# A fused attention and two-FFN kernel: first pass from one list in another order, 14 VectorE operations on GpSimd, later conversions at other steps

## The chip, the cores and the metric

The kernel runs on one core of one Trainium2 chip. The metric is the device time of one execution in microseconds (us); the kernel before takes 734.96 us, the median of three runs.

A core has five engines, each with its own queue of instructions that it works off in order: PE (TensorE) multiplies matrices, DVE (VectorE), ACT (ScalarE) and POOL (GpSimd) work on tiles, and SP (SyncE) here only starts DMA transfers. An engine waits at the head of its queue until the tiles that the instruction needs are ready and the buffers that it writes are free.

## The reference

Two softmax attentions in a row, then two feed-forward networks (FFNs):

```python
def sm_attn(qq, kk, vv):
    s = scale * np.matmul(qq, kk.transpose(0, 1, 3, 2))
    s = s - np.max(s, axis=-1, keepdims=True)
    a = np.exp(s)
    a = a / (np.sum(a, axis=-1, keepdims=True) + 1e-09)
    return np.matmul(a, vv)
p_packed = sm_attn(p, k, v)          # 32 packed tokens look at 576 tokens
out = sm_attn(q, p_packed, p_packed) # 576 tokens look at the 32 packed ones
...
x = ...reshape(B * S, H * D)         # 2304 tokens of 512 channels
g = softplus(x @ w_in);  x = g @ w_out        # first FFN, 2048 hidden channels
h = x @ w_in2;           h * sigmoid(h) @ w_out2   # second FFN, 2048 hidden channels
```

There are 4 batches, 8 heads of 64 channels and 576 tokens in a batch. `q`, `k`, `v`, `p` and the first FFN's `w_in` are drawn eight times as large as usual. All arrays are float32; the weights reach the kernel as 64-bit words, from which it makes float32.

## The kernel before

**Tiling.** The 2304 tokens are 8 blocks of 288 columns; block 2b and 2b + 1 belong to batch b. The first FFN's 2048 hidden channels are 16 tiles of 128, worked in 4 passes of 4 tiles: a unit is one block with the 4 hidden tiles of a pass (the first two blocks are cut into units of 2 tiles), a step is one hidden tile of a unit or one output tile of the unit before. There are 128 steps, 32 to a pass, so step 32 begins the second pass. One matrix instruction of PE is called a product.

**One step s of the first FFN.** `emit_in(s)` (L533) makes `h`, six products of 128x288: float32 accuracy comes from splitting each operand into a high part and a low part and multiplying three pairs. `act_scalar` (L550) has ACT take the softplus of `h` and round it to the high part `gh`; `act_vector` (L563) has DVE subtract for the low part `gl` (L564). `emit_out(s)` (L570) makes one output tile `y` of the unit before, twelve products (L596; in the first 8 steps plain float32 products from `gf`, L589). `finish_out` (L602) copies or adds `y` to the sum `ya` (L608 on ACT, L610 and L612 on DVE). `h` has two PSUM buffers, and so has `y`: the `h` of step s cannot start before the softplus and the `gl` of step s - 2 have read theirs. In the first 28 steps the softplus goes into a tile `gt`, so that the bank is free without `gl`; from step 28 on it stays in the bank, and the bank is free only when `gl` is made.

**Attention in the first pass.** `att1(b)` (L363) is the attention of batch b's packed tokens: scores of `kt` and `pz` (L376), two row maxima `top` (L382, DVE), two exponentials (L388, ACT), transposes through PE (L397) and their copies `et` (L402, L404, ACT), products with the values `vt` (L412), the division into `px` (L437 to L440, DVE), its transpose (L445) and the copy `pt` (L449). `att2(blk)` (L451) is the attention of a block: scores (L460), a transpose into `tr` and its maximum, difference, exponential, sum, a small addition, reciprocal and product (L469 to L483: DVE, the exponential ACT), the transpose `tb` (L485), its high part in `ax` (L490, ACT) and its low part (L492, DVE). `packed(b, qs)` (L500) multiplies the packed values with a part of `w_in` into `vw` (L509 PE, L517 ACT, L525 DVE); the FFN's `h` is then made from `ax` and `vw`. All of it shares two PSUM buffers, `psa`.

**Conversions.** `conv_w` (L155) makes float32 weights of the first FFN from raw words `wraw`: a scaling on ACT (L147, L149), a shift (L165) and one or two ORs (L168, L171) on DVE, and for `w_out` the high part on ACT (L183) and the low part `lo` (L186), on DVE at first, on POOL from step 32 on. From step 32 on the second FFN's weights are converted too and stored to DRAM for later: pairs of `w_in2` tiles (steps in the table `I2`; shift and OR L212 to L217 DVE, sums L231 POOL, high part L240 ACT, low part L246 POOL, store `wd` L254) and tiles of `w_out2` (table `O2`; sums L287 POOL, high part L272 ACT, low part L276 POOL, and for each second tile the rest L297 ACT and L301 POOL; stores `od` L280 and `td` L304). All loads and stores stand in SP's queue in the order in which they are written.

**What sets the order.** The order of each engine's queue is the order in which the program issues the operations. Each piece of work is a generator (`Item`) that stops at yields named after points of a step ("PE", "D1", "A1", ...). `start()` (L749) writes out the beginning by hand; `plan_all()` (L681) then puts items and loads on an agenda by step numbers, and `run_steps` (L813) goes through the steps and runs, at each point, all items that wait for it.

`warm(n)` (L739) issues n products of the identity with itself, filler work for PE; there are 54 of them in the first pass. After the 128 steps comes the second FFN (`second`), which the change does not touch.

Of the kernel before, what the change touches and what calls it, by code (L numbers as in the profile page):

```python
# [49 lines left out]
def body(ctx, tc, kT, vv, qT, pT, wi1, wo1, wi2, wo2, out):  # L50
# [26 lines left out]
    def setup():  # L77
        make_identity(nc, ident)
        nc.scalar.preload_act_table_set("exp_and_others")
# [14 lines left out]
    class Item:  # L94
# [9 lines left out]
        def first(self, point):  # L104
            assert self.due == point
            self.due = next(self.gen, None)
# [48 lines left out]
    def conv_w(k, n, signed=False):  # L155
# [29 lines left out]
        eng = nc.gpsimd if "x" in banks else nc.vector  # L185
# [152 lines left out]
    kts, vts, qts, pts = {}, {}, {}, {}  # L338

    def load_k(b):  # L340
        pz = att.tile([P, NK, NP], F32, name="pz", bufs=2)
        nc.sync.dma_start(out=pz, in_=pT[b])
        nc.gpsimd.tensor_scalar(out=pz, in0=pz, scalar1=SCALE, scalar2=None, op0=ALU.mult)
# [19 lines left out]
    def att1(b):  # L363
# [87 lines left out]
    def att2(blk, last=False):  # L451
# [18 lines left out]
        if blk == 3:  # L470
            yield "next"
# [7 lines left out]
        nc.vector.tensor_scalar(out=mx[:, 1], in0=mx[:, 1], scalar1=1e-9, scalar2=None, op0=ALU.add)  # L479
        nc.vector.reciprocal(out=mx[:, 1], in_=mx[:, 1])  # L480
        if blk == 2:
            yield "D2"
        nc.vector.tensor_tensor(out=tr, in0=tr, in1=mx[:, 1].unsqueeze(2).to_broadcast(wide), op=ALU.mult)  # L483
        tb = att.tile([P, NR, N0], F32, name="tb", bufs=1)
        nc.vector.transpose(tb, tr.rearrange("q (r g) p -> q r (g p)", r=NR))  # L485
        if last:
            yield "next"
# [4 lines left out]
        nc.vector.tensor_tensor(  # L492
# [7 lines left out]
    def packed(b, qs):  # L500
# [18 lines left out]
        if b == B - 1 and qs == (1,):  # L519
            yield "next"  # L520
            yield "D1"
        else:
            yield "D"
# [26 lines left out]
    def act_scalar(s, h):  # L550
# [7 lines left out]
        gt = h if s >= base(1) - 4 else att.tile([P, N0], F32, name="gt", bufs=2)  # L558
# [4 lines left out]
    def act_vector(s, gt, gh, gl):  # L563
        nc.vector.tensor_tensor(out=gl, in0=gt, in1=gh.bitcast(F32), op=ALU.subtract)  # L564
# [37 lines left out]
    def finish_out(u, dm, y):  # L602
# [3 lines left out]
        if u == FIRST[blk]:  # L606
            if dm % 2 or u < 3:
# [56 lines left out]
    I2 = (1, 4), (10, 13), (19, 22), (33, 34), (40, 44), (52, 54), (64, 69), (75, 78)  # L664
    O2 = 3, 6, 12, 15, 21, 25, 31, 36, 42, 46, 57, 62, 68, 70, 81, 83
# [15 lines left out]
    def plan_all():  # L681

        for n, s in (("i", 4), 11), (("i", 5), 19), (("i", 6), 26), (("i", 7), 28):
            when[n] = s
        for n, s in (("o", 4), 17), (("o", 5), 30), (("o", 6), 32), (("o", 7), 34):
            when[n] = s
        for f in range(1, NPASS - 1):
            for d, s in enumerate((5, 9, 26, 28)):
                when["i", GJ * f + GJ + d] = base(f) + s
            for d, s in enumerate((11, 17, 18, 24)):  # L690
                when["o", GJ * f + GJ + d] = base(f) + s
        for (k, n), s in when.items():
            ring = RING[k]
            free = last_use(k, n - ring) if n >= ring else 0
# [28 lines left out]
        for b in range(1, B):  # L723
            t = 8 * b
            if b > 1:
                plan_load(lambda b=b: load_k(b), t - 16)
                plan_load(lambda b=b: load_v(b), t - 13)
                plan(Item(att1(b)), (t - 10, t - 9, t - 7, t - 6, t - 5))
            for i in range(2):
                plan_load(lambda i=i, b=b: load_q(2 * b + i), max(0, t - 11 + i))  # L730
            plan(Item(att2(2 * b)), (t - 4, t - 3, t - 2))
            last = b == B - 1
# [540 lines left out]
```

## Time and profile before

| | |
|---|---|
| Three runs, median (lowest to highest) | 734.96 us (734.56 to 735.1) |
| The profiled execution, its own time | 735.33 us |
| Its span in the trace | 733.5 us |
| PE busy | 720.1 us, 98% of the span |
| DVE busy | 532.0 us, 73% |
| ACT busy | 395.3 us, 54% |
| POOL busy | 383.0 us, 52% |

The span is what the trace covers, from the first to the last instruction; 1.8 us of the execution's own time lie around it. The busy times of the engines overlap, so the share says only which engine has hardly any room. How long an engine stood still, and for whom, is in the list of waits; where that was is in the timeline, which shows instruction for instruction when it started, how long it took and, in brackets, how long its engine had stood still before it and what it had waited for.

### The profile page before, as it was taken

What the parts mean: (1) busy time and instruction counts of PE and PEld (TensorE: products, weight loads), DVE (VectorE), ACT (ScalarE), POOL (GpSimd) and SP (SyncE); (2) the same over time, 40 slices, a digit from 0 to 9 for tenths busy, and PEclk for the clock granted to TensorE, in tenths of its full rate; (3) what the DMA queues carried; (4) which work ended last, traced back from release to release, by engine and by line L of the source; (5) the groups of instructions that cost most, each with busy time, mean ns of one, the idle gap of its engine ahead of it and who ended that gap; (6) DMA issues with size and microseconds to landing.
All of it is one profiled execution on the core that took longest, in us unless ns stands there. A gap on an engine that the chain in (4) does not pass through costs nothing.

```text
span 733.5 us, 14136 instructions
## 1 busy us (share of the span) xinstructions
PE 720.1 (98%) x5336; PEld 686.9 (94%) x5336; DVE 532.0 (73%) x943; ACT 395.3 (54%) x785; POOL 383.0 (52%) x338
## 2 busy tenths in 40 slices
PE   8998999997999999999999999999999999999998
PEld 6776989997999999999999999999999999999997
DVE  3888888898878888855855567787567776745557
ACT  3667886766756657555535453544553353443341
POOL 0000000558736836447007657679766769865655
PEclk9999999999999999999999999999999999999999
DMA  8965060567787584562928978788987787897842
GB/s 335 359 229 180 9 258 2 202 232 287 285 303 271 236 324 185 202 245 88 369 81 255 311 238 276 238 259 269 324 263 245 245 265 244 300 309 234 257 127 101
DMA packets 78915, 173.22 MB, mean 236 GB/s; under 512 B 6400, under 2 KB 52992, under 8 KB 76288
## 3 DMA queue, kind: packets, MB, share of 16 engines
q1 hardware_dynamic: 78848, 172.33, 68.9%
q8 instruction: 42, 0.69, 0.4%
q14 instruction: 25, 0.20, 0.1%
HBM read 136.13 MB, written 36.18 MB: 235 GB/s over the span
## 4 chain that ended last, share of the span: by engine, by line
PE 78%; DVE 11%; ACT 4%; DMA 2%; issue 2%; POOL 1%; SPq 0%; DVEq 0%; POOLq 0%
PE y L976 23%; PE y L596 18%; PE h L547 9%; PE pB L919 7%; PE pA L919 7%; PE pC L919 7%; PE pD L919 3%; PE psa L509 2%; DVE wx L165 1%; PE y L589 1%; DMA wraw<-wi 1%; DMA td<-tmp 1%; DVE gl L564 1%; DVE raw L214 1%; DVE wx L168 1%
## 5 line engine op out<-in xcount | busy, mean ns | idle before, releaser
L596 PE MATMUL y<-gh,w 128*128 128x288 f32 x960 | 211.9, 297 | 0.2 <-DVE ya L610 0.2
L596 PEld LDWEIGHTS y<-gh,w 128*128 128x128 f32 x960 | 160.3, 188 | 12.8 <-issue 11.8
L976 PE MATMUL y<-G,w 128*128 128x384 f32 x840 | 164.4, 334 | 0.2 <-DVE acc L991 0.2
L976 PEld LDWEIGHTS y<-G,w 128*128 128x128 f32 x840 | 147.2, 188 | 0.5 <-DVE acc L991 0.5
L596 PE MATMUL y<-gl,w 128*128 128x288 f32 x480 | 141.4, 295 | 0.0
L547 PE MATMUL h<-ax,vw 128*128 128x288 f32 x768 | 125.1, 299 | 5.4 <-DVE gl L564 4.5
L547 PEld LDWEIGHTS h<-ax,vw 128*128 128x128 f32 x768 | 108.8, 188 | 9.1 <-DVE gl L564 6.3
L958 POOL TENSOR_TENSOR G<-sums,G 128x384 fp32r<-128x384 f32 x76 | 87.9, 1178 | 35.1 <-ACT G L954 21.0
L950 POOL TENSOR_TENSOR sums<-tmp 128x384 f32<-128x384 f32 x47 | 56.5, 1224 | 91.9 <-ACT tmp L1163 90.6
L596 PEld LDWEIGHTS y<-gl,w 128*128 128x128 f32 x480 | 90.1, 188 | 0.0
L559 ACT ACTIVATE h<-h 128x288 f32<-128x288 f32 x100 | 38.9, 389 | 50.6 <-PE h L547 48.3
L564 DVE TENSOR_TENSOR gl<-h,gh 128x288 fp32r<-128x288 f32 x100 | 45.0, 450 | 28.4 <-ACT gh L560 28.3
L186 POOL TENSOR_TENSOR w<-wx,w 128x512 fp32r<-128x512 f32 x10 | 14.0, 1402 | 93.7 <-ACT w L183 93.7
L1159 ACT ACTIVATE tmp<-tmp 128x384 f32<-128x384 f32 x24 | 12.6, 526 | 80.5 <-DVE tmp L1090 80.5
L1090 DVE TENSOR_TENSOR tmp<-tmp,pB 128x384 f32<-128x384 f32 x48 | 26.4, 550 | 40.2 <-PE pB L919 36.1
L612 DVE TENSOR_TENSOR ya<-y,ya 128x288 f32<-128x288 f32 x104 | 46.6, 450 | 10.2 <-PE y L596 10.2
L1090 DVE TENSOR_TENSOR G<-tmp,G 128x384 fp32r<-128x384 f32 x61 | 45.4, 745 | 11.4 <-ACT G L1160 6.1
L287 POOL TENSOR_TENSOR tmp<-tmp 128x256 f32<-128x256 f32 x32 | 23.8, 755 | 50.0 <-DVE tmp L217 25.5
L1119 ACT ACTIVATE tmp<-pA 128x384 f32<-128x384 f32 x24 | 11.8, 492 | 68.3 <-PE pA L919 68.3
L919 PE MATMUL pC<-xc,w 128*128 128x384 f32 x240 | 48.1, 334 | 0.0
L919 PE MATMUL pB<-xc,w 128*128 128x384 f32 x240 | 48.1, 334 | 0.0
L991 DVE TENSOR_TENSOR ya<-y,ya 128x384 f32<-128x384 f32 x70 | 38.4, 552 | 11.1 <-PE y L976 10.8
(144 smaller groups left out, 1399.4 us busy)
## 6 DMA issues: line engine op xcount, KB each, us to landing
w<-wd SPq DMA_DIRECT2D x84, 512.0 KB, 4.5
w<-td SPq DMA_DIRECT2D x96, 256.0 KB, 3.9
w<-od SPq DMA_DIRECT2D x72, 256.0 KB, 4.1
wd<-whl SPq DMA_DIRECT2D x8, 1792.0 KB, 8.8
wraw<-wi SPq DMA_DIRECT2D x16, 512.0 KB, 6.3
wraw<-wo SPq DMA_DIRECT2D x16, 512.0 KB, 9.1
raw<-wi SPq DMA_DIRECT2D x16, 512.0 KB, 6.1
raw<-wo SPq DMA_DIRECT2D x16, 512.0 KB, 5.3
```

Source lines behind the costliest of these rows:

```text
L287: sub = lambda o, a, b: nc.gpsimd.tensor_tensor(out=o, in0=a, in1=b, op=ALU.subtract)
L547: nc.tensor.matmul(h, lhsT=w, rhs=x, start=(i == 0), stop=(i == len(mm) - 1))
L559: nc.scalar.activation(out=gt, in_=h, func=AF.Softplus)
L564: nc.vector.tensor_tensor(out=gl, in0=gt, in1=gh.bitcast(F32), op=ALU.subtract)
L596: nc.tensor.matmul(y, lhsT=w[:, c], rhs=g, start=(j == js[0] and m == 0), stop=(j == js[-1] and m == 2))
L612: nc.vector.tensor_tensor(out=acc, in0=y, in1=acc, op=ALU.add)
L919: nc.tensor.matmul(out, lhsT=a, rhs=b, start=start and not i, stop=not start and i == len(mm) - 1, skip_group_check=True,)
L950: eng.tensor_tensor(out=sum_of(q), in0=a, in1=b, op=op)
L958: eng.tensor_tensor(out=u[:, 1], in0=sum_of(q), in1=u[:, 0].bitcast(F32), op=ALU.subtract)
L976: nc.tensor.matmul(y, lhsT=w, rhs=g, start=not m, stop=m == len(mm) - 1)
L991: vec = lambda o, x, z, op=ALU.add: nc.vector.tensor_tensor(out=o, in0=x, in1=z, op=op)
L1090: add = lambda o, i, j, op=ALU.add: nc.vector.tensor_tensor(out=o, in0=i, in1=j, op=op)
```

## The change

The first pass (steps 0 to 31 and what comes ahead of them) is no longer planned by steps. One list, `SCRIPT`, has a token for each operation or next stage of an item, in the order in which they are issued: `a1.b` is the next stage of `att1(b)`, `a2.k` of `att2` of block k, `v.b.i` of `packed`, `w.k.n` of `conv_w`; `in.s`, `sp.s`, `gl.s`, `out.s` and `fin.u.d` are `emit_in`, softplus and rounding, `gl`, `emit_out` and `finish_out`; `L...` are loads, `warm.n` is filler, `table` is the load of ACT's first table. New yields let stages that were one be issued apart. The first batch's `pz` is loaded through ACT's queue instead of SP's, and the table load now stands behind it.

Fourteen operations of DVE go to POOL (`ON_POOL`): the difference `sub` of blocks 2, 4, 5, 6 and 7, the product `mul` of blocks 2 and 5 and the low part `low` of blocks 0 and 2 (nine of 128x576), `lo` of weight 3 (128x512), `gl` of steps 14 and 21 (128x288), and the small addition `eps` of blocks 4 and 7. Which first copies of `y` go to ACT is now a list, `BY_SCALAR`; two more of them are on DVE than before.

From step 32 on, the conversions of weights for the last two passes move: in the second and the third pass the `w_in` tiles from steps 5, 9, 26, 28 to 7, 9, 26, 29 and the `w_out` tiles from 11, 17, 18, 24 to 11, 19, 17, 24. In the tables of the second FFN's weights six of the eight pairs in `I2` and two tiles in `O2` have other steps, and the store of a pair is asked for one step later.

```diff
     def setup():
         make_identity(nc, ident)
-        nc.scalar.preload_act_table_set("exp_and_others")
...
-        eng = nc.gpsimd if "x" in banks else nc.vector
+        eng = nc.gpsimd if "x" in banks else engine("lo", n)
...
+    def load_p(b):
+        pz = pzs[b] = att.tile([P, NK, NP], F32, name="pz", bufs=2)
+        (nc.sync if b else nc.scalar).dma_start(out=pz, in_=pT[b])
+        nc.gpsimd.tensor_scalar(out=pz, in0=pz, scalar1=SCALE, scalar2=None, op0=ALU.mult)
...
-        nc.vector.tensor_tensor(out=tr, in0=tr, in1=mx[:, 0].unsqueeze(2).to_broadcast(wide), op=ALU.subtract)
+        yield "D2" if blk == 3 else "D"
+        engine("sub", blk).tensor_tensor(out=tr, in0=tr, in1=mx[:, 0].unsqueeze(2).to_broadcast(wide), op=ALU.subtract)
...
-        nc.vector.tensor_tensor(
+        engine("low", blk).tensor_tensor(
             out=ax[:, NR:, cols], in0=tb, in1=ax[:, :NR, cols].bitcast(F32), op=ALU.subtract
         )
...
-        gt = h if s >= base(1) - 4 else att.tile([P, N0], F32, name="gt", bufs=2)
+        gt = h if s >= IN_BANK else att.tile([P, N0], F32, name="gt", bufs=2)
...
-        nc.vector.tensor_tensor(out=gl, in0=gt, in1=gh.bitcast(F32), op=ALU.subtract)
+        (engine("gl", s) if s < IN_BANK else nc.vector).tensor_tensor(out=gl, in0=gt, in1=gh.bitcast(F32), op=ALU.subtract)
...
-            if dm % 2 or u < 3:
+            if 4 * u + dm in BY_SCALAR:
...
-    I2 = (1, 4), (10, 13), (19, 22), (33, 34), (40, 44), (52, 54), (64, 69), (75, 78)
-    O2 = 3, 6, 12, 15, 21, 25, 31, 36, 42, 46, 57, 62, 68, 70, 81, 83
+    I2 = (1, 5), (10, 13), (20, 22), (32, 34), (42, 44), (52, 54), (65, 66), (72, 75)
+    O2 = 3, 6, 12, 15, 21, 25, 30, 36, 45, 46, 57, 62, 68, 70, 81, 83
...
-            for d, s in enumerate((5, 9, 26, 28)):
+            for d, s in enumerate((7, 9, 26, 29)):
                 when["i", GJ * f + GJ + d] = base(f) + s
-            for d, s in enumerate((11, 17, 18, 24)):
+            for d, s in enumerate((11, 19, 17, 24)):
                 when["o", GJ * f + GJ + d] = base(f) + s
...
-            plan_load(lambda jp=jp: store_i(jp), b + 7)
+            plan_load(lambda jp=jp: store_i(jp), b + 8)
...
+    ON_POOL = (("sub", 4), ("lo", 3), ("sub", 7), ("low", 2), ("sub", 6), ("mul", 2), ("sub", 2), ("gl", 21), ("low", 0), ("sub", 5), ("gl", 14), ("eps", 4), ("mul", 5), ("eps", 7), )
+    IN_BANK = 28
+    BY_SCALAR = (0, 1, 2, 3, 4, 5, 6, 17, 22, 25, 27, 30, 31, 32, 33, 34, 35, 36)
+    engine = lambda *x: nc.gpsimd if x in ON_POOL else nc.vector
...
+        warm.12 Lp.0 table.exp_and_others Lk.0 Lw.i.0 Lv.0 Lw.i.1 Lq.0 Lw.o.0 Lw.o.1 a1.0 Lp.1 Lq.1 Lk.1
+        Lw.i.2 Lw.i.3 Lw.o.2 Lw.o.3 w.i.0 a1.0 w.i.0 w.i.0 a1.0 a1.0 a1.0 warm.8 a1.0 a1.0 a1.0 a1.0 a1.0
...
     with tc.manual_schedule():
-        start()
         plan_all()
+        first_pass()
         run_steps(NS)
```

In the fences below a row is an instruction of the engine's queue with its line, its tiles (the number behind a name tells tiles of the same name apart) and the size that it writes; x4 stands for four such in a row.

At the very start DVE's queue makes the row maxima of batch 0 (`sm`, L382), two float32 weights (`wx` and `wraw`, L165 and L171) and the packed values `px`. Before:

```order
L382 TENSOR_REDUCE sm_123<-psa_138 128x1
L382 TENSOR_REDUCE sm_123<-psa_139 128x1
L165 TENSOR_SCALAR wx_175<-wraw_110 128x512
L171 SCALAR_TENSOR_TENSOR wraw_110<-wraw_110,wx_175 128x512
L165 TENSOR_SCALAR wx_251<-wraw_115 128x512
L437 TENSOR_SCALAR sm_123<-psa_209 128x2
L438 RECIPROCAL sm_123<-sm_123 128x2
L440 TENSOR_TENSOR px_255<-psa_209,sm_123 128x128
L171 SCALAR_TENSOR_TENSOR wraw_115<-wraw_115,wx_251 128x512
```

Now, with the same lines under other numbers (L384 is the maximum, L164 the shift, L170 the OR, L443 to L446 `px`), in DVE's queue:

```order
L384 TENSOR_REDUCE sm_103<-psa_140 128x1
L164 TENSOR_SCALAR wx_176<-wraw_127 128x512
L170 SCALAR_TENSOR_TENSOR wraw_127<-wraw_127,wx_176 128x512
L384 TENSOR_REDUCE sm_103<-psa_141 128x1
L443 TENSOR_SCALAR sm_103<-psa_211 128x2
L444 RECIPROCAL sm_103<-sm_103 128x2
L446 TENSOR_TENSOR px_255<-psa_211,sm_103 128x128
L164 TENSOR_SCALAR wx_257<-wraw_132 128x512
L170 SCALAR_TENSOR_TENSOR wraw_132<-wraw_132,wx_257 128x512
```

The second weight's shift has moved from ahead of `px` to behind it, and the first weight's shift and OR from behind the second maximum to ahead of it.

At batch 2 PE's queue has the scores of `att1(2)` (L376), the transposes of its two exponentials (L397, `e_723` and `e_725`), and around them `h` (L547) and `y` (L589) of the first steps. Before:

```order
L376 MATMUL psa<-kt,pz 32x288 x16
L589 MATMUL y<-gf,wraw 128x288 x4
L547 MATMUL h<-ax,vw 128x288 x12
L589 MATMUL y<-gf,wraw 128x288 x2
L547 MATMUL h<-ax,vw 128x288 x6
L589 MATMUL y<-gf,wraw 128x288 x2
L397 MATMUL psa<-ident,e_723 128x128 x4
L397 MATMUL psa<-ident,e_723 64x128
L397 MATMUL psa<-ident,e_725 128x128 x4
L397 MATMUL psa<-ident,e_725 64x128
L547 MATMUL h<-ax,vw 128x288 x6
L589 MATMUL y<-gf,wraw 128x288 x2
```

Now (L378 scores, L399 transposes, L546 `h`, L588 `y`, L414 the products with the values), in PE's queue:

```order
L378 MATMUL psa<-kt,pz 32x288 x16
L546 MATMUL h<-ax,vw 128x288 x12
L588 MATMUL y<-gf,wraw 128x288 x2
L399 MATMUL psa<-ident,e_726 128x128 x4
L399 MATMUL psa<-ident,e_726 64x128
L588 MATMUL y<-gf,wraw 128x288 x2
L399 MATMUL psa<-ident,e_728 128x128 x4
L399 MATMUL psa<-ident,e_728 64x128
L546 MATMUL h<-ax,vw 128x288 x6
L588 MATMUL y<-gf,wraw 128x288 x2
L546 MATMUL h<-ax,vw 128x288 x6
L414 MATMUL psa<-vt,et 32x65 x40
```

Four products of `y` have moved from behind the scores to ahead of them, one `h` of six products from ahead of the transposes to behind them, and two products of `y` stand between the transposes.

At steps 49 to 52, in the second pass, DVE's queue has `gl` (L564), the sum `ya` (L612) and the conversions of weights for the third pass (L165 to L171). Before:

```order
L165 TENSOR_SCALAR wx_2375<-wraw_2196 128x512
L168 SCALAR_TENSOR_TENSOR wx_2375<-x_2349,wx_2375 128x512
L171 SCALAR_TENSOR_TENSOR wx_2375<-x_2349,wx_2375 128x512
L564 TENSOR_TENSOR gl_2359<-h_2351,gh_2358 128x288
L612 TENSOR_TENSOR ya_92<-y_2362,ya_92 128x288
L165 TENSOR_SCALAR wx_2414<-wraw_2233 128x512
L168 SCALAR_TENSOR_TENSOR wx_2414<-x_2388,wx_2414 128x512
L171 SCALAR_TENSOR_TENSOR wx_2414<-x_2388,wx_2414 128x512
L564 TENSOR_TENSOR gl_2398<-h_2390,gh_2397 128x288
L612 TENSOR_TENSOR ya_92<-y_2401,ya_92 128x288
```

Now (L164 to L170 the conversion, L563 `gl`, L611 `ya`), in DVE's queue:

```order
L164 TENSOR_SCALAR wx_2375<-wraw_2195 128x512
L167 SCALAR_TENSOR_TENSOR wx_2375<-x_2349,wx_2375 128x512
L170 SCALAR_TENSOR_TENSOR wx_2375<-x_2349,wx_2375 128x512
L563 TENSOR_TENSOR gl_2359<-h_2351,gh_2358 128x288
L611 TENSOR_TENSOR ya_92<-y_2362,ya_92 128x288
L563 TENSOR_TENSOR gl_2396<-h_2388,gh_2395 128x288
L611 TENSOR_TENSOR ya_92<-y_2399,ya_92 128x288
L164 TENSOR_SCALAR wx_2440<-wraw_2274 128x512
L167 SCALAR_TENSOR_TENSOR wx_2440<-x_2414,wx_2440 128x512
L170 SCALAR_TENSOR_TENSOR wx_2440<-x_2414,wx_2440 128x512
L563 TENSOR_TENSOR gl_2424<-h_2416,gh_2423 128x288
```

The second of the two conversions has moved back by one step: a step without a conversion now lies between them.

## Rows read from the trace of the kernel before

**Rows 1.** Page, part 1: each engine's busy us (share of the span) xinstructions

```profile
PE 720.1 (98%) x5336; PEld 686.9 (94%) x5336; DVE 532.0 (73%) x943; ACT 395.3 (54%) x785; POOL 383.0 (52%) x338
```

**Rows 2.** Waits of PE: line waited for: us in total, times, longest us

```profile
PE h L547 <- DVE gl L564: 4.5, 5, 2.0
...
PE psa L445 <- DVE px L440: 1.0, 1, 1.0
PE h L547 <- ACT gt L559: 1.0, 1, 1.0
PE psa L509 <- DVE vw L525: 0.8, 1, 0.8
PE psa L412 <- ACT et L404: 0.4, 1, 0.4
```

**Rows 3.** Timeline, 13 to 126 us: start, us, engine, line, out<-in [idle before <-releaser]

```profile
13.31 0.43 DVE L165 TENSOR_SCALAR wx<-wraw 128x512 int32<-128x512 int32 x1 [2.93 <-DMA wraw<-wi]
...
14.48 0.30 PE L445 MATMUL psa<-ident,px 128*128 128x128 f32 x1 [1.01 <-DVE px L440]
...
123.27 0.95 PE L547 MATMUL h<-ax,vw 128*128 128x288 f32 x6
...
125.64 0.95 PE L547 MATMUL h<-ax,vw 128*128 128x288 f32 x6
```

**Rows 4.** Timeline of PE and ACT, 48 to 60 us

```profile
48.56 1.43 PE L376 MATMUL psa<-kt,pz 64*32 64x288 f32 x32
49.92 2.21 PE L589 MATMUL y<-gf,wraw 128*128 128x288 f32 x8
...
56.75 1.28 ACT L559 ACT_TABLE_LOAD   x1
...
58.51 1.06 PE L547 MATMUL h<-ax,vw 128*128 128x288 f32 x6 [0.96 <-ACT gt L559]
```

**Rows 5.** Timeline of SP's queue and of POOL, 153 to 163 us

```profile
153.60 0.38 SPq L304 DMA_DIRECT2D td<-tmp  x1
...
162.16 0.74 POOL L287 TENSOR_TENSOR tmp<-tmp 128x256 f32<-128x256 f32 x1 [4.72 <-DMA td<-tmp]
```

**Rows 6.** Timeline, 168 to 184 us

```profile
171.20 0.69 DVE L168 SCALAR_TENSOR_TENSOR wx<-x,wx 128x512 int32<-128x512 int32 x1 [2.26 <-ACT x L149]
...
173.03 1.06 PE L547 MATMUL h<-ax,vw 128*128 128x288 f32 x6 [1.34 <-DVE gl L564]
...
173.08 2.39 POOL L301 TENSOR_TENSOR tmp<-tmp 128x1024 fp32r<-128x1024 f32 x1
...
173.26 2.49 DVE L165 TENSOR_SCALAR wx<-wraw 128x512 int32<-128x512 int32 x1
...
177.69 1.07 PE L547 MATMUL h<-ax,vw 128*128 128x288 f32 x6 [2.02 <-DVE gl L564]
...
180.97 1.06 PE L547 MATMUL h<-ax,vw 128*128 128x288 f32 x6 [0.63 <-DVE gl L564]
```

**Rows 7.** DVE by line and shape, 0 to 124 us: xcount | busy us, mean ns | idle

```profile
L564 DVE TENSOR_TENSOR gl<-gt,gh 128x288 fp32r<-128x288 f32 x20 | 8.8, 441 | 3.0 <-ACT gh L560 3.0
...
L474 DVE TENSOR_TENSOR tr<-tr,mx 128x576 f32<-128x576 f32 x8 | 6.1, 758 | 0.3
...
L186 DVE TENSOR_TENSOR w<-wraw,w 128x512 fp32r<-128x512 f32 x4 | 2.7, 673 | 0.0
```

**Rows 8.** POOL by line and shape, whole span

```profile
L276 POOL TENSOR_TENSOR ohl<-tmp,ohl 128x512 fp32r<-128x512 f32 x16 | 21.8, 1365 | 0.0
L301 POOL TENSOR_TENSOR tmp<-tmp 128x1024 fp32r<-128x1024 f32 x8 | 19.4, 2431 | 0.3 <-ACT tmp L297 0.3
...
L343 POOL TENSOR_SCALAR pz<-pz 128x128 f32<-128x128 f32 x4 | 2.5, 620 | 45.6 <-DMA pz<-pT 45.6
```

**Rows 9.** Instructions of L165 and L1090: ns min/median/max, first and last start

```profile
L165 DVE TENSOR_SCALAR wx<-wraw x32: 385/418/2656, 9.2 to 281.5; 128x512 int32<-128x512 int32 x32
...
L1090 DVE TENSOR_TENSOR G<-tmp,G x61: 546/559/1412, 378.5 to 707.3; 128x384 fp32r<-128x384 f32 x61
```

More of the change, by code (lines that the diff above doesn't have):

```diff
@@ L102, in run, with step @@
                     self.due = next(self.gen, None)
-        def first(self, point):
-            assert self.due == point
+        def step(self):
+            assert self.due
             self.due = next(self.gen, None)
@@ L423, in att1 @@
         exp(0)
+        yield "A1"
         exp(1)
@@ L518, in packed @@
             vs.append(v)
[L519 to L523, printed above, removed]
+        yield "D"
         for i, (q, v) in enumerate(zip(qs, vs)):
@@ L693, in plan_all @@
             ring = RING[k]
-            free = last_use(k, n - ring) if n >= ring else 0
+            free = last_use(k, n - ring)
             load = max(s - 5, free)
@@ L721, in plan_all @@
             plan_load(lambda r=r: load_s(r), base(3) + 24)
[L723 to L732, printed above, removed]
-            plan(Item(att2(2 * b + 1, last)), (t - 3,) + (t - 2,) * (b == 1) + (t - 1, t) + (t + 1,) * last)
         for (b, qs), s in vstep.items():
-            plan(Item(packed(b, qs)), (s, s + 1) if b == B - 1 and qs == (1,) else (s,))
+            if s >= base(1):
+                plan(Item(packed(b, qs)), (s,))
     def warm(n):
@@ new lines, in body, with first_pass, act, send @@
+    """
+    def first_pass():
+        items, made, ys = {}, {}, {}
+        for b in range(B):
+            items[f"a1.{b}"] = Item(att1(b))
+            for i in range(2):
+                items[f"a2.{2 * b + i}"] = Item(att2(2 * b + i))
+                items[f"v.{b}.{i}"] = Item(packed(b, (i,)))
+        items["v.0.2.3"] = Item(packed(0, (2, 3)))
+        for n in range(2 * GJ):
+            for k in "io":
+                items[f"w.{k}.{n}"] = Item(conv_w(k, n, n < 2 + (k == "i")))
+        def act(s):
+            made[s] = act_scalar(s, made[s])
+        def send(s):
+            for y in emit_out(s):
+                ys[y[:2]] = y
+        calls = {
+            "Lp": load_p, "table": nc.scalar.preload_act_table_set, "Lk": load_k, "Lv": load_v, "Lq": load_q, "Lw": load_w, "warm": warm, "sp": act, "out": send,
+            "in": lambda s: made.update({s: emit_in(s)}), "gl": lambda s: act_vector(s, *made[s]),
+            "fin": lambda u, dm: finish_out(*ys.pop((u, dm))),
+        }
+        for t in SCRIPT.split():
+            if t in items:
+                items[t].step()
+            else:
+                name, *args = t.split(".")
+                calls[name](*(int(a) if a.isdigit() else a for a in args))
+        assert not ys
+        for k, n, s in LATE:
+            plan(items[f"w.{k}.{n}"], s)
@@ L813, in run_steps @@
     def run_steps(end):
-        for s in range(end):
+        for s in range(base(1), end):
             if s == base(1):
@@ L835, in run_steps @@
             r = act_scalar(s, h)
[L836 removed]
+            ys = emit_out(s)
             go("PE2")
[L838 to L844 removed]
             go("A1")
```

129 lines of the change are left out of this document (36 added, 93 removed).

## The prediction, made before the changed kernel was run

> **What bounds the kernel now.** I read the busy table first: the matrix unit PE is busy for 98% of the span, so this is a kernel of one engine, and a change can give only what PE idles or does needlessly [rows 1]. The change adds and drops no matrix instruction: the same tiles are multiplied, and the 54 filler products of `warm` stay 54. So the next view is the list of what PE waited for [rows 2]. Its rows are the whole purse: 4.5 us in five waits for `gl`, and some 4 us of waits of a microsecond or less. Those small ones lie in the first pass, which ends where PE begins step 32, at 123.27 us; the `gl` waits lie behind it [rows 2, 3]. A kernel with none of these waits would be 8 to 9 us faster, no more.
>
> Then I read the places in order of time. At 13 to 15 us VectorE (DVE) stands 2.93 us for a weight's DMA, and the small operations that make `px` stand behind that in DVE's queue; PE waits 1.01 us for `px` [rows 3]. At 48 to 59 us the scores of batch 2 are done at 49.99, yet PE waits 0.96 us at 58.51 for a softplus: DVE comes to the row maxima late, so ScalarE's exponentials are late, and the table load of 1.28 us and the softplus come behind them [rows 4]. Shortly behind it stands a wait of 0.4 for `et`, and at 70 us one of 0.8 for `vw` [rows 2].
>
> The large hole is in the second pass. GpSimd (POOL) waits 4.72 us for the store of `td`, issued at 153.60, and goes on at 162.16 [rows 5]. Its sums are then late; ScalarE waits for them and is late with the scaled weight; DVE waits 2.26 us for that weight, and `gl`, which stands behind it, frees PE's bank 1.34 us too late. Then two weight conversions follow in neighbouring steps (49 and 50), and the shift of the second takes 2.49 us: it ends only when POOL's operation of 2.39 us, begun at 173.08, has ended. For that PE waits 2.02 and 0.63 us more [rows 6]. The two other `gl` waits, 4.5 − 3.99 = 0.5 us together [rows 2], come behind such shifts in the third pass and later.
>
> **The change part by part.** *Fourteen operations from DVE to POOL.* Nine are of 128x576, one of 128x512, two of 128x288, two tiny. By DVE's rows that takes 9 × 0.758 + 0.673 + 2 × 0.441 = 8.4 us off DVE [rows 7]. Two more copies of `y` come to DVE from ScalarE, at `gl`'s size about 0.9 us. POOL has no such operation before step 32; its nearest rows are 1.365 us for 128x512 and 2.431 for 128x1024, so I estimate 1.50 for 576 columns and 0.9 for 288: 9 × 1.50 + 1.4 + 1.8 = 16.7 us, in a stretch where it had only the four scalings of `pz` to do [rows 8]. Each result comes 0.75 us later than DVE would give it, and is hidden only where its consumer is late anyway.
>
> *Another order of the first pass.* (a) Start: `px` now stands ahead of the shift that waits for the DMA, and two filler products fill the time until then. Against that, the first weight's shift and OR (a median of 0.42 us [rows 9], and about 0.67 as `lo` of that width) now stand between the two row maxima, which delays the second exponential. Bounds: the whole 1.01 us gained, or 0.5 lost. I take 0.2 gained. (b) Batch 2: between the scores and the `h` that waited, the order drops four `y` products (eight records, 2.2 us) and moves one `h` group behind; the 7.6 us of PE work there (49.99 to 58.51 less 0.96) becomes some 4.6 to 4.9 [rows 4]. What must fit in is the chain of two maxima, the second exponential, table load and softplus. I count maxima and exponential like DVE's operations of 576 columns and the softplus like `gl`: 3 × 0.76 + 1.28 + 0.44 = 4.0 us, if DVE is free when the scores end. It is: four 576-column operations have left its queue ahead of the maxima and one copy has come in, 4 × 0.758 − 0.44 = 2.6 us net, and the scores come 2 us later. So the 0.96 us goes, and the 0.4 for `et` behind it; the cover left is under 1 us. (c) The wait of 0.8 for `vw`: PE arrives earlier by what (b) gave, DVE's queue from `px` to it is about 1 us shorter; I take 0.3 of it as gained, bounds 0 and 0.8. (d) New: the `h` of batch 3's first block (block 6) hangs on a copy, table load, softplus, rounding, `ax` and its low part: 3 × 0.44 + 1.28 + 2 × 0.76 = 4.1 us behind the product that starts the chain. PE now has two products and an `h` for it, also some 4 us: 0.3 us lost, bounds 0 and 1. Sum of the first pass: 0.2 + 1.0 + 0.4 + 0.3 − 0.3 = 1.6 us, bounds −1.1 (the start 0.5 worse, `et` and `vw` as before, (b) eaten up by (d) and as much again elsewhere) and 3.2.
>
> *Conversions at other steps.* The two conversions of steps 49 and 50 become 49 and 51 (the same distance apart in the third pass). The `td` store stands behind the same raw load in SyncE's queue, so POOL's late start stays, and with it the first 1.34. But step 50 is now free of a conversion, so DVE catches up ahead of the next shift: the 2.02 and 0.63 go. In their place come four conversions in a row at steps 51 to 54, under POOL's same long operations. A step of PE has 125.64 − 123.27 = 2.37 us [rows 3]; one with a conversion needs 0.42 + 2 × 0.67 + 2 × 0.44 = 2.6 of DVE. I put 0.8 us of new waiting there, bounds 0 and 4. The 0.5 of the later places goes, less 0.1. Sum: 2.65 − 0.8 + 0.4 = 2.25 us, bounds −1.4 and 4.5.
>
> *Nothing* I give to the table load and the load of `pz` that now stand in ScalarE's queue: the twelve filler products cover both. Nothing either to the loads moved in SyncE's queue: the closest is the key tile of batch 3, asked for when batch 2's values are used up, at some 62 us, and needed at some 73; without that cover it would cost what it lands late.
>
> DVE work on SBUF tiles beside a busy POOL is the price I trust least. The trace shows it: the shift has a median of 418 ns and a maximum of 2656, and a product of two SBUF tiles 546 at least and 1412 at most [rows 9]. The Trainium skill, "SBUF — State Buffer", section "Who interferes with whom", says that DVE operations with two SBUF inputs or in a two-port mode and GpSimd operations lock each other out for a whole instruction; the two maxima agree. By that rule the moved operations could cost more than they free; that is rival 4. I place them by the order: most run while DVE reads PSUM or reduces, which in this trace stays at its length.
>
> **The rivals.** 1. *Forecast:* 1.6 + 2.25 = 3.85 us off 735.33 us, the profiled execution's own time: 731.48. It stands 0.37 above the median of 734.96, so 731.1. Chance 0.55.
> 2. *Nearly all waits go:* `td` lands earlier, since the large store of `wd` is now asked for later, and the first 1.34 goes too, and `vw` fits. First pass 2.8, later 4.3: 734.96 − 7.1 = 727.9. For it: POOL's chain is at the bound only by that DMA [rows 5]. Chance 0.17.
> 3. *One half only:* the hole moves from steps 51–53 to 53–55 at its size, since the shifts meet POOL there; only the first pass gains: 734.96 − 1.6 = 733.4. Chance 0.17, about half of it faster.
> 4. *Slower by the lock:* ten long moved operations each hold a two-operand DVE operation (OR, `lo`, `ax` low) for most of their 1.5 us. At 1.0 each DVE gets 10 us for 8.4 it gave away and 0.9 more of copies, and the chains are 0.75 longer. From where DVE stands over 2.5 us behind PE, the two `h` banks are used up and each microsecond is PE's: about 2.5 us lost in the first pass, nothing net later: 737.5. Against it: beside most of the moved operations DVE's queue holds work that reads PSUM or reduces. Chance 0.06.
> 5. *No change:* PE's order only trades its waits, 735. Chance 0.05.
>
> **How the numbers follow.** The forecast's own bounds, its less certain terms at their nearer ends, are 729 to 732.8. The range reaches into case 2 and most of case 3: 727.6 to 733.7, leaving out some 0.2. The measurement tells 0.2% (1.5 us) from no change. Faster by more: 0.55 + 0.17 + 0.08 = 0.80; the same 0.09 + 0.05 = 0.14; slower 0.06.
>
> **What would show it.** In the changed kernel's list of PE's waits: no softplus wait near 57 us; `px` at about half a microsecond or more still; a `gl` wait of about 1.3 us near 171 us, none of 2 us. PE should start step 32 at about 121.7 us. POOL operations of 576 columns at 1.4 to 1.6 us. I am wrong if such an operation takes over 2 us with DVE standing, if a `gl` wait of 2 us stands at steps 53 to 56, or if step 32 starts later than 123.

## The result and the profile after

The changed kernel takes **728.56 us**, the median of four runs (727.86 to 729.4), against 735.03 for the kernel before beside it (734.56 to 736.12): a ratio of 0.991, 95% interval 0.9893 to 0.9928, or 6.5 us faster. The predicted 731.1 had the right sign and the range held the time, but the gain is 1.7 times the forecast one. The profiled executions compared below are 735.33 and 727.86 us, spans 733.5 and 726.1: 7.4 us apart. That is about 1 us more than the medians are apart, since the profiled execution of the kernel before lies above its median and that of the changed kernel is the fastest of its four.

The page's first part after the change, to set against [rows 1]:

```profile
PE 717.5 (99%) x5336; PEld 686.7 (95%) x5336; DVE 521.9 (72%) x931; ACT 394.7 (54%) x783; POOL 396.8 (55%) x352
```

The same 5336 matrix instructions occupy PE for 2.6 us less (720.1 before). That is the first surprise: the prediction counted only what PE idles. What PE waits for after the change (line waited for: us in total, times, longest), against [rows 2]:

```profile
PE h L546 <- DVE gl L563: 2.1, 2, 1.5
...
PE psa L399 <- ACT e L390: 0.9, 1, 0.9
PE psa L466 <- ACT pt L455: 0.4, 1, 0.4
PE psa L451 <- DVE px L446: 0.3, 1, 0.3
```

The waits for the softplus, for `et` and for `vw` are gone, and those for `gl` fell from 4.5 to 2.1 us. Three waits at the start stand in the place of one.

PE begins step 32 here:

```profile
118.19 0.95 PE L546 MATMUL h<-ax,vw 128*128 128x288 f32 x6
```

Before it was 123.27 [rows 3]. So 5.1 us of the 7.4 are made in the first pass and 2.3 behind it; the forecast was 1.6 and 2.25. The table of windows cut at that step tells where the 5.1 us were (from and to, us, then busy us and instructions of PE, of the weight loads PEld, of DVE, ACT and POOL, the granted clock as a share of full speed, DMA share, GB/s). Before:

```profile
0.00:123.27 123.27, 117.82 (x1357) 98.31 (x1358) 98.04 (x186) 85.87 (x162) 3.16 (x10) 1.00 0.56 204
```

After:

```profile
0.00:118.19 118.19, 115.30 (x1357) 98.10 (x1357) 90.80 (x175) 84.00 (x159) 17.18 (x24) 1.00 0.56 209
```

PE's idle time fell from 5.45 to 2.89 us, 2.56 less. The other 2.52 us were busy time of the same 1357 matrix instructions. The weight loads show the whole of it: PEld works 98 us in both, and what it does not work fell from 24.96 to 20.09 us, by 4.87. That says that the pass lost no work, not where the time was. The page on traces in the Trainium skill ("Perfetto Trace Analysis", section "Identifying the Most-Contended Engine") says that the busy share of matrix products is not a good measure of how near a kernel is to what the engine can do, and names the busy share of the weight loads as one of two measures to use instead; these two rows agree.

A place where it can be seen: batch 2. Here the timeline of PE before, from the first `h` behind the scores' `y` products to the transpose of `px`:

```profile
51.75 1.97 PE L547 MATMUL h<-ax,vw 128*128 128x288 f32 x12
...
64.44 0.30 PE L445 MATMUL psa<-ident,px 128*128 128x128 f32 x1
```

And after, with the scores:

```profile
50.49 1.20 PE L378 MATMUL psa<-kt,pz 64*32 64x288 f32 x32
51.62 1.85 PE L546 MATMUL h<-ax,vw 128*128 128x288 f32 x12
...
56.26 1.03 PE L546 MATMUL h<-ax,vw 128*128 128x288 f32 x6
...
61.46 0.27 PE L451 MATMUL psa<-ident,px 128*128 128x128 f32 x1
```

The same 32 score products take 1.43 us in [rows 4] and 1.20 here, with no idle time before either. The records of these products of 64x32 overlap (one takes 0.40 us or a little more, all 32 of them 1.20), so when one of them waits the others cover it in the record, and the group only looks longer. No list names what the products of batch 2 waited for. At batch 1 the same group shows it: before

```profile
22.19 1.71 PE L376 MATMUL psa<-kt,pz 64*32 64x288 f32 x32
```

and after

```profile
22.25 1.20 PE L378 MATMUL psa<-kt,pz 64*32 64x288 f32 x32
```

In the list of what the weight loads waited for there is a row for this place in the kernel before, which PE's own list does not have:

```profile
PEld psa L376 <- DVE tr L469: 0.4, 1, 0.4
```

### The profile page after: what moved, and what is told of

Read it like the earlier page. It is cut to its first block, busy times and chain, and to the rows that moved or that the text cites. A ratio compares the mean times of both kernels' runs of the same rounds, so it can differ in the third digit from the quotient of the medians.

```text
span 726.1 us, 14132 instructions
## 1 busy us (share of the span) xinstructions
PE 717.5 (99%) x5336; PEld 686.7 (95%) x5336; DVE 521.9 (72%) x931; ACT 394.7 (54%) x783; POOL 396.8 (55%) x352
## 4 chain that ended last, share of the span: by engine, by line
PE 93%; DVE 3%; DMA 1%; POOL 1%; ACT 1%; issue 1%; SPq 0%; DVEq 0%; POOLq 0%
PE y L595 24%; PE y L952 23%; PE h L546 13%; PE pB L895 7%; PE pA L895 7%; PE pC L895 7%; PE pD L895 3%; PE y L588 2%; PE psa L512 2%; PE y L728 2%; DMA td<-tmp 1%; PE psa L414 1%; PE psa L378 1%; PE psa L466 1%; PE psa L399 1%
## 5 line engine op out<-in xcount | busy, mean ns | idle before, releaser
L546 PE MATMUL h<-ax,vw 128*128 128x288 f32 x768 | 123.8, 298 | 2.2 <-DVE gl L563 2.1
L546 PEld LDWEIGHTS h<-ax,vw 128*128 128x128 f32 x768 | 108.2, 188 | 6.1 <-DVE gl L563 3.0
L563 DVE TENSOR_TENSOR gl<-h,gh 128x288 fp32r<-128x288 f32 x100 | 45.2, 452 | 29.7 <-ACT gh L559 29.7
L611 DVE TENSOR_TENSOR ya<-y,ya 128x288 f32<-128x288 f32 x104 | 46.7, 451 | 10.9 <-PE y L595 10.1
L1066 DVE TENSOR_TENSOR tmp<-tmp,pC 128x384 f32<-128x384 f32 x48 | 26.5, 553 | 26.2 <-PE pC L895 25.1
L559 ACT ACTIVATE gh<-h 128x288 fp32r<-128x288 f32 x100 | 41.2, 412 | 3.2
```

The costliest lines, as they stand in the source:

```text
L546: nc.tensor.matmul(h, lhsT=w, rhs=x, start=(i == 0), stop=(i == len(mm) - 1))
L559: nc.scalar.activation(out=gh, in_=gt, func=AF.Copy)
L563: (engine("gl", s) if s < IN_BANK else nc.vector).tensor_tensor(out=gl, in0=gt, in1=gh.bitcast(F32), op=ALU.subtract)
L611: nc.vector.tensor_tensor(out=acc, in0=y, in1=acc, op=ALU.add)
L1066: add = lambda o, i, j, op=ALU.add: nc.vector.tensor_tensor(out=o, in0=i, in1=j, op=op)
```

## The experiments

The times stand beside the kernel before on the same chip in the same job: 735.44 us for `first_only`, `later_only`, `none_on_pool` and `before_on_pool`; 735.31 for `after_again`, `i_28`, `o_18` and `store_9`; 735.26 for `pool_0_2` and the three kernels with `raw_last` in their names.

### The halves apart

`first_only` is the changed kernel with the old steps from step 32 on; `later_only` is the kernel before with the new ones.

```diff
-    I2 = (1, 5), (10, 13), (20, 22), (32, 34), (42, 44), (52, 54), (65, 66), (72, 75)
-    O2 = 3, 6, 12, 15, 21, 25, 30, 36, 45, 46, 57, 62, 68, 70, 81, 83
+    I2 = (1, 4), (10, 13), (19, 22), (33, 34), (40, 44), (52, 54), (64, 69), (75, 78)
+    O2 = 3, 6, 12, 15, 21, 25, 31, 36, 42, 46, 57, 62, 68, 70, 81, 83
...
-            for d, s in enumerate((7, 9, 26, 29)):
+            for d, s in enumerate((5, 9, 26, 28)):
...
-            for d, s in enumerate((11, 19, 17, 24)):
+            for d, s in enumerate((11, 17, 18, 24)):
...
-            plan_load(lambda jp=jp: store_i(jp), b + 8)
+            plan_load(lambda jp=jp: store_i(jp), b + 7)
```

(`later_only` is the same diff the other way round, made in the kernel before.)

> The changed kernel with the later conversions (I2, O2, the steps of w_in and w_out tiles, the pair store) back at the steps of before. Theory A, from the two traces: step 32 begins 5.1 us earlier (123.27 to 118.19) and the rest of the gain is made later, so this keeps about 5 us of it: 730.0. Theory B, the split of the prediction (1.6 us in the first pass): 733.4. PE begins step 32 at 118.2 by A, and the holes of 1.3, 2.0 and 0.6 us behind gl at steps 51 to 53 are back by both.

Measured: 730.14 us, 0.9933 of the kernel before (0.9921 to 0.9946), 5.3 us faster. PE begins step 32 at 118.39.

> The kernel before with the later conversions alone at the steps of the change. The forecast put 2.25 us there and the traces show 2.3: both say 732.7. If the halves depend on each other (the holes at steps 51 to 53 go only when DVE enters step 32 with less work behind it), it gains under 1 us: 734.2.

Measured: 733.05 us, 0.9966 (0.9954 to 0.9979), 2.4 us faster. PE's waits for `gl`:

```profile
PE h L547 <- DVE gl L564: 2.7, 2, 1.4
```

They were 4.5 in five [rows 2]. The halves are nearly independent, theory A holds, and the prediction's 1.6 us for the first pass was too small by a factor of three.

### Order or relief

`none_on_pool` keeps the new list and takes the fourteen operations back; `before_on_pool` has the old order and the fourteen operations on POOL.

```diff
-    ON_POOL = (("sub", 4), ("lo", 3), ("sub", 7), ("low", 2), ("sub", 6), ("mul", 2), ("sub", 2), ("gl", 21), ("low", 0), ("sub", 5), ("gl", 14), ("eps", 4), ("mul", 5), ("eps", 7), )
+    ON_POOL = ()
```

and, in the kernel before, with the same list, at each of the six places where one of them is issued:

```diff
-        nc.vector.tensor_tensor(out=tr, in0=tr, in1=mx[:, 0].unsqueeze(2).to_broadcast(wide), op=ALU.subtract)
+        engine("sub", blk).tensor_tensor(out=tr, in0=tr, in1=mx[:, 0].unsqueeze(2).to_broadcast(wide), op=ALU.subtract)
```

> The changed kernel, same list, but all fourteen operations on VectorE again. Theory O, the order alone makes the first pass shorter: DVE has 27 us idle there, so under 1 us is lost, 729.0. Theory R, the relief of DVE makes it: 8.4 us come back onto DVE between 15 and 115 us, where PE follows it closely, and 3 us or more are lost, 731.5 to 733.5.

Measured: 732.38 us, 0.9957 (0.9945 to 0.997). Of the 5.1 us of the first pass 4.5 are gone: step 32 begins at 122.68. The order of PE's instructions is the changed kernel's, so the two traces can be laid side by side. Three places stand out, all in its timeline:

```profile
29.82 4.15 PE L588 MATMUL y<-gf,wraw 128*128 128x288 f32 x16 [1.01 <-ACT gf L552]
...
48.00 1.24 PE L588 MATMUL y<-gf,wraw 128*128 128x288 f32 x4 [0.59 <-ACT ya L607]
...
52.39 0.99 PE L588 MATMUL y<-gf,wraw 128*128 128x288 f32 x3 [0.58 <-DVE ya L611]
```

With the fourteen on POOL these products began at 28.46, at 44.82 and 48.46 in groups without a break. The list was put together for a DVE with 8 us less work.

> The kernel before in its own order, with the same fourteen operations on GpSimd. Theory R (relief): the waits for softplus, et and vw go, 2 to 3 us faster, 732.5. Theory O (order): the chains become 0.4 us longer at each moved operation, the waits stay, 735.0 within 0.7. The lock of the prediction's fourth rival: slower, 737.

Measured: 734.19 us, 0.9986 (0.9974 to 0.9997), 1.2 us faster by the medians and 1.0 by the ratio, with an interval that ends just short of no change. The softplus and `et` waits stay (0.9 and 0.7 us); only `vw`'s is gone. So neither half of the first pass does much alone: 0.6 us by the order (123.27 to 122.68) and 0.9 by POOL (to 122.37), 5.1 together. These are single traces, and one and the same first pass began step 32 at 118.19 and 117.84 in two traces of the changed kernel, at 123.27 and 122.90 in `before` and `later_only`; so the two small numbers are rough, and the large one is not in doubt. Both theories as I put them fall short; it is the combination.

### Which of the fourteen

`pool_0_2` leaves four on POOL:

```diff
+    ON_POOL = ("low", 0), ("sub", 2), ("mul", 2), ("low", 2)
```

> The changed kernel with only four of the fourteen operations on GpSimd: the low part of blocks 0 and 2, the difference and the product of block 2. Without any of the fourteen, PE lost 1.1 us at 28 us and 0.75 and 0.85 us at 46 and 49 us, in all 2.7 of 4.5 us before batch 2. If these four stand behind these three places, the 2.7 us are back and 1.8 us are lost: 729.9. If it is the sum of DVE's work that counts, four of eleven longer operations give back about a third, 1.6 us: 730.8.

Measured: 729.24 us, 0.992 (0.9906 to 0.9933). In the first pass it loses 1.0 us to the changed kernel (step 32 at 119.16) where `none_on_pool` loses 4.5: the four operations that stand ahead of 50 us bring 3.5 of it, not in proportion to DVE's work but because DVE is what PE follows there. The three waits above are gone.

### The stall that PE's list does not show

Beside the gains the traces have a loss: between steps 62 and 63 the changed kernel gives back 0.8 us, with no wait in PE's list. The timeline of PE and of the weight loads there:

```profile
197.48 1.92 PE L512 MATMUL psa<-wraw,pt 64*32 64x512 f32 x16
...
198.35 0.14 PEld L512 LDWEIGHTS psa<-wraw,pt 64*32 64x32 f32 x4 [0.70 <-DVE wraw L170]
```

and the same product before:

```profile
204.65 1.09 PE L509 MATMUL psa<-wraw,pt 64*32 64x512 f32 x16
```

The fourth `w_in` tile is now converted one step later, and the last quarter of this product waits for it. `i_28` puts it back:

```diff
-            for d, s in enumerate((7, 9, 26, 29)):
+            for d, s in enumerate((7, 9, 26, 28)):
```

> The changed kernel with the fourth w_in tile converted at step 28 of a pass again instead of 29. Theory W: at step 62 the product that makes vw waits for that tile in the middle of its group (1.92 us for the group instead of 1.09 in the trace of before), a stall that PE's list of waits does not show; it goes, and 0.8 us are gained: 727.8. Rival: the 0.8 us stands on PE's way only in the record, 728.6.

`after_again`, the changed kernel beside it:

> The changed kernel once more, as it is, so that the next three have it beside them on one chip: 728.6 by all theories.

Measured: `after_again` 728.08 us (727.51 to 728.56), `i_28` 727.65 (727.07 to 728.15): the times overlap and do not tell the two apart. The trace does at the place:

```profile
197.97 1.09 PE L512 MATMUL psa<-wraw,pt 64*32 64x512 f32 x16
```

The product is back at 1.09 us and the 0.8 is regained there, so the stall was real; some 0.3 us are lost ahead of it, at step 62, where PE now waits 0.16 us for a `gl` that stands behind the moved conversion in DVE's queue.

### The hole at steps 51 to 53

After the change the hole reads as follows (SP's queue, then POOL, DVE and PE in the timeline):

```profile
147.41 0.38 SPq L303 DMA_DIRECT2D td<-tmp  x1
```

```profile
155.80 0.75 POOL L286 TENSOR_TENSOR tmp<-tmp 128x256 f32<-128x256 f32 x1 [4.55 <-DVE gl L563]
```

```profile
166.67 1.05 PE L546 MATMUL h<-ax,vw 128*128 128x288 f32 x6 [0.63 <-DVE gl L563]
...
169.12 1.83 POOL L245 TENSOR_TENSOR whl<-wf,whl 128x768 fp32r<-128x768 f32 x1
...
169.16 2.09 DVE L164 TENSOR_SCALAR wx<-wraw 128x512 int32<-128x512 int32 x1
...
173.18 1.06 PE L546 MATMUL h<-ax,vw 128*128 128x288 f32 x6 [1.49 <-DVE gl L563]
```

To set against [rows 5, 6]: `td` still takes 8.4 us from issue to the end of POOL's wait (8.6 before), but it is issued 1.1 us earlier against PE's steps, POOL starts 0.7 earlier against them, and the first wait is 0.63 in place of 1.34. The 2.02 and 0.63 are gone, and 1.49 is new. 2.1 us in all; the prediction had 1.34 + 0.8. (The releaser `gl` that POOL's row names had long been done; in `after_again`, with the same instructions, the row names the DMA of `td`.)

Two kernels test the prediction's two reasons. `o_18` puts the second `w_out` tile at step 18, so that conversions stand in the neighbouring steps 49 and 50 again; `store_9` asks for the large store `wd` one step later, to free the DMA for `td`.

```diff
-            for d, s in enumerate((11, 19, 17, 24)):
+            for d, s in enumerate((11, 18, 17, 24)):
```

> The changed kernel with the second w_out tile converted at step 18 of a pass instead of 19, so that two conversions stand in neighbouring steps (49 and 50) as before the change. The forecast's mechanism: waits for gl of 2.0 and 0.6 us are back at steps 52 and 53, and the 1.5 at step 53 goes: about 1.1 slower, 729.7. Rival, the hole only moves with the shift that meets POOL's long operation: 728.6 within 0.4.

Measured: 728.48 us (727.74 to 729.4), not told apart from `after_again`. Its trace has the wait at step 52:

```profile
171.53 1.38 PE L546 MATMUL h<-ax,vw 128*128 128x288 f32 x6 [1.85 <-DVE gl L563]
```

and none at step 53; it begins step 54 2.1 us behind `after_again`. So the place of the wait is as forecast: with a free step between the two conversions it is not at step 52. Its price is not. Of the 2.1 us 0.3 stood already at step 32, and the two `gl` waits of the stretch, 2.85 us here and 2.4 in `after_again`, differ by 0.4. The rest is PE's clock. Behind the wait PE worked for 0.7 us, and then the granted clock was 0.50, the lower of its two levels (1.2 GHz, not 2.4). Columns as in the table of windows above:

```profile
172.20:175.05 2.85, 2.85 (x13) 2.85 (x13) 2.30 (x5) 1.57 (x4) 1.55 (x2) 0.50 0.13 52
```

At half the clock 2.85 us do the work of some 1.4, an estimate that fills the gap. 1.2 of the 2.1 us come back up to step 63, most of it because the product above then has its weights in time, and the total does not show the difference.

The same happened in the trace of `first_only`, behind a wait of 2.06 us (clock 0.50 from 172.9 to 176.3 us), and not behind the 2.02 us in the trace of the kernel before:

```profile
177.69:181.00 3.31, 2.68 (x19) 2.45 (x19) 3.10 (x6) 2.62 (x7) 2.42 (x2) 1.00 0.30 124
```

The mean clock of each execution, on record for the changed kernel and for all executions of the experiments, tells how often. One such drop takes some 0.002 off the mean (0.5 × 2.85 of 727 us, an estimate). The mean was 0.998 in 24 of 51 executions of the four kernels that have a `gl` wait of 1.85 us or more (the kernel before, `first_only`, `before_on_pool`, `o_18`), and 0.999 or more in all 43 of the others. In the kernel before the 15 executions at 0.998 have a median of 735.64 us and the 16 others 734.86. So a part of what the change gives by the medians is likely this clock; the two profiled executions compared above do not have it.

```diff
-            plan_load(lambda jp=jp: store_i(jp), b + 8)
+            plan_load(lambda jp=jp: store_i(jp), b + 9)
```

> The changed kernel with the store of a pair asked for one step later still (9 steps behind the second conversion instead of 8). Theory D: td takes 8.4 us to land since the 1792 KB of wd follow it by 1.7 us; with wd 2.4 us later td lands 1 us or more earlier, POOL starts earlier and the 0.63 at step 51 goes: 727.9. Rival: td is held up by what stands ahead of it (raw, od) and the loads, 728.6.

Measured: 728.5 us (727.88 to 728.87). `wd` is issued 2.9 us behind `td` in place of 1.7, and `td` still takes 8.6 us (147.54 to 156.09): theory D falls. What stands ahead of `td` in SP's queue does it. Here that queue in `after_again`:

```profile
135.24 0.33 SPq L202 DMA_DIRECT2D raw<-wi  x1
146.20 0.33 SPq L202 DMA_DIRECT2D raw<-wo  x1
146.62 0.39 SPq L279 DMA_DIRECT2D od<-ohl  x1
147.10 0.38 SPq L303 DMA_DIRECT2D td<-tmp  x1
```

and what the DMA engines moved from 135 to 160 us, in 40 slices of 0.625 us:

```profile
GB/s 354 426 413 420 393 105 7 0 0 0 0 0 0 0 0 0 0 0 0 92 170 164 288 354 459 419 452 419 341 361 406 442 446 531 482 367 367 413 328 416
```

For 11 us the queue stands, and for 7 of them nothing moves. What SP's queue waited for there:

```profile
SPq L202 <- DVE wf L216: 10.6, 1, 10.6
```

A raw load at its head waits until DVE has read the ring buffer that it is to fill, and the finished stores `od` and `td` stand behind it. When it goes, 2 MB want to move at once. The next kernels write the raw loads of a step behind its stores, and change nothing else; once in the changed kernel and once in the kernel before.

```diff
-        for m, (s, k, n) in enumerate(use):
-            free = use[m - RAW][0] if m >= RAW else 0
-            plan_load(lambda k=k, n=n: load_raw(k, n), base(1) + max(free, s - 5))
...
                 plan_load(lambda n=n: t_store(n), s + 4)
+        for m, (s, k, n) in enumerate(use):
+            free = use[m - RAW][0] if m >= RAW else 0
+            plan_load(lambda k=k, n=n: load_raw(k, n), base(1) + max(free, s - 5))
```

> The changed kernel with one thing else: of the transfers that are written at one step, the loads of the second FFN's raw words now stand behind the stores od and td in SyncE's queue, not ahead of them. Theory Q: no transfer moves between 139 and 146 us because a raw load at the head of SyncE's queue waits for its ring buffer, and td, whose data POOL has ready by 144.5, stands behind it; now td is issued by 145 and POOL's sums start at 151.7, when DVE has their input, not at 155.8; POOL's long operations come 1.3 us earlier, so the 0.6 to 0.9 us wait at step 51 goes and the shift at step 51 is held 1 us less: 1.5 to 2 us faster than the changed kernel, 726.3. Rival: the raw loads then come late for DVE elsewhere, no gain or a loss, 728.1 to 730.

Measured: **725.94 us** (725.66 to 725.96), 0.9875 of the kernel before (0.986 to 0.989), and 2.1 us under `after_again` (of another job). Between steps 50 and 54 it gains 2.5 us on `after_again`, and later it gives back 0.4. The three steps of the theory in its timeline:

```profile
141.77 0.33 SPq L303 DMA_DIRECT2D td<-tmp  x1
```

```profile
151.58 0.74 POOL L286 TENSOR_TENSOR tmp<-tmp 128x256 f32<-128x256 f32 x1 [0.57 <-POOL w L185]
...
167.60 0.47 DVE L164 TENSOR_SCALAR wx<-wraw 128x512 int32<-128x512 int32 x1
...
167.76 2.02 POOL L245 TENSOR_TENSOR whl<-wf,whl 128x768 fp32r<-128x768 f32 x1
```

`td` leaves 5.6 us earlier, POOL starts its sums as soon as DVE has made their input, and the shift now slips in ahead of POOL's long operation: 0.47 us, not 2.09. Its `gl` waits are 0.6 us in all.

> The kernel before with the raw loads behind the stores od and td in the same way, nothing else. Theory Q: the first wait of 1.34 us at step 51 goes, and POOL's long operation is over earlier when the shift of step 50 comes, so of the 2.0 and 0.6 us behind it about 1 us goes too: 733.0. Rival (the hole is made by conversions in neighbouring steps, whenever td lands): only the 1.3 goes or moves, 734.1 to 735.4.

Measured: 732.6 us, 0.9965 (0.9953 to 0.9978), 2.7 us faster than the kernel before; the five `gl` waits of 4.5 us are four of 2.2. Of the 2.7, 2.5 are gained between steps 50 and 54, though raw loads at other steps moved too. The place of a load in the queue was worth as much in the kernel before as all the moved conversions of the change (2.4).

> The changed kernel with the raw loads behind od and td and the fourth w_in tile at step 28 again. If the two gains add (1.5 to 2, and 0.4 for step 28 as measured): 725.9. If the conversions at steps 57 to 60 collide with what POOL now does earlier: as raw_last alone, 726.3 or more.

Measured: 726.15 us (725.85 to 726.66), no better than `raw_last`: the gains don't add, and of the kernels run here `raw_last` has the lowest median.

## Why the prediction was right, and where it was not

**The sign and the bound held.** PE was the bound, the gain came from what PE lost, and no lock between DVE and POOL cost what was gained.

**The step that failed is the first one: "its rows are the whole purse".** PE's list of waits has only idle time. Half of what the first pass gave, 2.52 of 5.08 us, lay inside groups that counted as busy. The first pass's sum of 1.6 with a bound of 3.2 was therefore too small from the start. By its terms:

- The start: forecast 0.2 gained, measured 0.06 lost (the 28 filler records begin at 16.24 before and at 16.30 after). The price named there, a second exponential delayed by the shift and the OR ahead of the second maximum, came in full: waits of 0.9 for `e` and 0.4 for `pt` beside 0.3 for `px`.
- From there to batch 2: no term of the forecast; 1.1 gained. At 51.75 and 51.62 us the two kernels stand behind the same work, but for one `h` of 0.95 us that the changed one has done in addition, and the start's 0.06 is caught up. `none_on_pool` shows what this rests on: it loses 2.7 us at three places of this stretch, and the four early operations of `pool_0_2` give them back. The scores of batches 1 and 2, 0.51 and 0.23 us shorter, are part of it.
- Batch 2: forecast 1.4, measured 1.9. From the rows above, (64.44 − 61.46) is 2.98, less the 1.1 gained up to there. The softplus and `et` waits, 1.4 together, are gone as forecast; the other 0.5 lay inside groups that counted as busy.
- `vw` and the stretch to the scores of batch 3: forecast 0.3, measured 1.2 (73.82 and 70.58, with one `h` of 0.95 more done). The wait of 0.8 went whole.
- The new wait at block 6: forecast 0.3 lost; it isn't there, and the last stretch gained 0.9.

**The price of the moved operations** was right for DVE, and on POOL a little high, 14.4 us in all against 16.7. POOL's groups in the first pass of the changed kernel:

```profile
L479 POOL TENSOR_TENSOR tr<-tr,mx 128x576 f32<-128x576 f32 x5 | 5.8, 1160 | 31.1 <-DVE mx L477 31.1
L495 POOL TENSOR_TENSOR ax<-tb,ax 128x576 fp32r<-128x576 f32 x2 | 2.8, 1414 | 6.9 <-ACT ax L493 6.9
L487 POOL TENSOR_TENSOR tr<-tr,mx 128x576 f32<-128x576 f32 x2 | 2.3, 1160 | 6.9 <-DVE mx L485 6.9
...
L563 POOL TENSOR_TENSOR gl<-gt,gh 128x288 fp32r<-128x288 f32 x2 | 1.6, 810 | 2.6 <-ACT gh L559 2.6
L185 POOL TENSOR_TENSOR w<-wraw,w 128x512 fp32r<-128x512 f32 x1 | 1.3, 1282 | 8.5 <-ACT w L182 8.5
```

What failed is that these 8 us were given no worth beyond the named waits. The order and the relief were priced one after the other, and each alone is in fact worth under 1 us; together they are worth 5.1. Of the prediction's own signs, `px` (0.3 us) and step 32 (118.19, not 121.7) came out better than it said; operations of 576 columns took 1.16 and 1.41 us on POOL, not 1.4 to 1.6.

**The conversions** came out at 2.3 of 2.25 us, and that this fits so well is luck. Right: POOL starts late again, the 2.02 and 0.63 go, and a new wait comes in their place. Wrong by size: the first wait is 0.63, not 1.34, and the new one 1.49, not 0.8; the two errors cancel to 0.02. Not foreseen: 0.6 gained at steps 44 to 47, 0.6 lost from 54 to 61, 0.8 lost at step 62 and 0.2 at 73, and that the places from step 82 on gave 1.3 in place of 0.4, again more than their idle time (0.24 and 0.25). PE's clock, which `o_18` shows behind the 2 us wait, is no term of the forecast either.

**The rivals.** The time came out near rival 2 (727.9), but not by its mechanism: `td` took as long as before. Rival 4 did not come, and the reason given against it is what the trace shows: in the first pass POOL's operations lie beside work of DVE that reads PSUM or reduces. It also counted the OR among what POOL holds up, and that the traces do not bear out (below). Rival 3 is refuted by `first_only` and `later_only`, which both gain.

## What to carry to other kernels

Where one engine is the bound, its list of waits is the least that it loses: compare the same group of instructions at several places (1.43 against 1.20, 1.92 against 1.09), and read the waits of the weight loads too. Here an order and the engine that each operation runs on belonged together, and one without the other said little, so try them together. Before conversions are moved to make room, look at the transfer queue: a load that waits for its buffer holds up every finished store behind it. And where two variants differ by a wait, look at the granted clock behind it before the whole difference is put down to the wait.

## What the runs showed of the hardware

A shift of 128x512 on DVE that starts just behind a long operation of POOL is held until that operation is over: 169.16 to 171.25 us, beside 169.12 to 170.95 on POOL. The rule of the Trainium skill that the prediction named ("SBUF — State Buffer", section "Who interferes with whom") agrees for the shift. New to me was that one tiny operation is held the same way. DVE's addition of 128x18, at 0.18 us in the median, here took 0.64:

```profile
94.95 0.64 DVE L484 TENSOR_SCALAR mx<-mx 128x18 f32<-128x18 f32 x1
```

POOL worked on a difference of 128x576 until 95.56. The operations with two SBUF inputs, which the rule names too, hardly ever lay beside POOL's in the first pass. Behind step 32 they do, and they are not alike. An operation on two float32 tiles is held at times: `G` from `tmp` and `G` [rows 9] took 549 to 559 ns in the 17 cases with POOL idle, and up to 1412 beside it. The OR of two tiles of 32-bit integers is not, though in 8 of these 18 POOL had begun first and still had over 0.6 us to go (nanoseconds, least, median and most, in the kernel before):

```profile
L168 DVE SCALAR_TENSOR_TENSOR wx<-x,wx x18: 690/692/693, 124.4 to 283.4; 128x512 int32<-128x512 int32 x18
```

So for the OR the rule does not hold in this case; why is open.

PE's clock is the other fact: in two traces it fell to half for some 3 us behind a wait of about 2 us in the middle of dense work, and each time PE had worked for under 1 us again when it fell.
